# First-phase results written from the chunk's own token tile by SyncE, k.v of a batch in one run, another prologue order

## The chip, the cores and the metric

The kernel runs on one core of one Trainium2 chip. The metric is device time in microseconds (us), the median over runs. In the text PE is TensorE, PEld its weight load, DVE is VectorE, ACT is ScalarE, POOL is GpSimd and SP is SyncE; "q" behind an engine's name (SPq) means its sequencer, which issues transfers.

## The reference, cut to what matters

```python
kv  = einsum('bhsd,bhse->bhde', k, v)            # 8 batches, 8 heads, 576 tokens, 64 features
o   = einsum('bhsd,bhde->bhse', q, kv)
o   = o / sqrt(mean(o*o, -1) + 1e-6) * g_norm
x   = o as (4608 tokens, 512)
x2  = ((x @ w1) * (x @ w2)) @ w3 @ w_out         # w1, w2: 512x1024, w3: 1024x1024, w_out: 1024x512
out = silu(x2 @ w_in) @ w_out2                   # w_in: 512x2048, w_out2: 2048x512
```

The inputs q, k, v are float32, and the weights are float64, read as pairs of 32-bit words. Products of the layers are split into a high and a low float32r part and take three matmuls each.

## The kernel before

The 4608 tokens are nine chunks of 512. The core works in three stages.

- **Prologue.** w3 @ w_out is folded into one 1024x512 matrix (the tiles `wch`, `wcl`), and attention of chunk 0 and k.v of batches 0 and 1 are made beside it. The order of everything here is the string `ORDER`: each word is one load, conversion (`scale`, `tail`, `bits`, `high`, `low`), matmul group (`hh`, `hl`, `lh`, `kmm`, `a`, `b`) or copy. A `tail` is done on ACT, a `tailv` on DVE.
- **First phase** (the loop from line 834 of the kernel before). The five chunks in `PLAIN` (0, 1, 3, 5, 7) go through the first layer in steps, eight steps (j) to a chunk, 40 in all. A step is twelve matmuls into `pa`, twelve into `pb`, and twelve into four banks `x2ps` for the step before. With the last step of a chunk, which is issued during the first step of the next chunk, the four banks are copied out by ACT and DVE in turn (lines 702 and 704) and written to `x2d`. The chunk's tokens stand in `xh` and `xl`, two buffers each. Beside the steps runs the attention of the later chunks, at points that the table `TIMES` gives in sixths of a step: `l` and `q` are loads of k, v and q, `k0` and `k3` are the matmuls of k.v of one batch (tiles 0 to 2, then 3 and 4, with the copy to `kv`), `a` is q times kv, `c` to `r` are the norm, and `f0` and `f1` hand on the result: into `xh` and `xl` for a chunk of `PLAIN`, or to DRAM (`xd`) for the chunks in `LATER` (2, 4, 6, 8). `PACE` says how many pieces of the later weights are converted in each third of a step; `advance` does one, and first issues the writes that wait in the list `writes` (`flush`, line 329).
- **Second phase.** The rest, in Strassen blocks of seven products (line 924). Its tables `LATES`, `RUNS` and `NEED` set its order.

Every engine takes its instructions strictly in the order in which they are written down, and SP and POOL issue transfers in that order as well, so a transfer that has to wait for a buffer or for data holds up all behind it on the same engine. A tile has as many buffers as `bufs` says: in the kernel before `k` and `v` have three each, `q` four, and `x2o`, the tile of the copied-out results, three for four results of a chunk. The loads and most writes are on SP; the writes to `xd` and, but for the last chunk, to `x2d` are on POOL.

Of the kernel before, what the change touches and what calls it, by code (L numbers as in the profile page):

```python
# [7 lines left out]
F32 = mybir.dt.float32  # L8
F32R = mybir.dt.float32r
U32 = mybir.dt.uint32  # L10
# [5 lines left out]
P = 128  # L16
B, H, S, D = 8, 8, 576, 64
DM = H * D
# [28 lines left out]
""" if x.isdigit())  # L47
TIMES = {
# [47 lines left out]
load0 load1 load2 kload0 scale0 tail0 load3 scale1 scale2 bits0 tailv1 highv0 tailv2 bits1 low0 kmm0  # L96
high1 kload1 low1 hh1 lh1 bits2 qload0 scale3 tail3 highv2 load4 kload2 low2 kmm1 bits3 scale4
hl1 tail4 qload3 highv3 kload3 lh2 kmm2 low3 qload2 qload1 kload4 bits4 high4 hh2 hl2 low4
hl3 kmm3 kmm4 kout0 load5 scale5 tailv5 lh3 bits5 load6 a0 b0 highv5 load7 low5 scale6
tailv6 bits6 scale7 hh3 load8 tail7 highv6 low6 bits7 a1 lh5 b1 high7 load9 scale8 hh5  # L100
c0 tailv8 hl5 hl7 low7 lh7 scale9 tailv9 load10 bits8 d0 bits9 kload5 hh7 load11 high8
scale10 tailv10 low8 load12 high9 e0 hh8 lh8 low9 eh0 bits10 load13 el0 scale11 tail11 high10
bits11 hl8 hl10 r0 low10 hh10 kload6 scale12 load14 tailv12 gload0 highv11 bits12 high12 low11 x0
lh10 lh11 load15 load16 scale13 low12 tail13 r1 hh11 bits13 x1 hl11 highv13 fh0 scale14 tail14
bits14 kload7 hl13 kmm5 scale15 fh1 kmm6 low13 tailv15 scale16 lh13 kload8 hh13 wh0 wh4 wh1
highv14 bits15 low14 kmm7 kload9 high15 wl0 wl1 low15 wh5 kmm8 kmm9 tail16 wl5 lh14 kout1
bits16 hl15 hl14 wl4 fl1 hh14 lh15 hh15 highv16 low16 fl0
# [4 lines left out]
def fused(ctx, tc, q, k, v, g, w1, w2, w3t, wo1, wb, out):  # L112
# [241 lines left out]
    def kv_load(b, js):  # L354
        for j in js:
            n = min(P, S - j * P)
            for nm, src in (("k", k), ("v", v)):
                t = at.tile([P, DM], F32, tag=nm, bufs=3, name=f"{nm}{b}_{j}")
                nc.sync.dma_start(out=t[:n], in_=src[b, j * P:j * P + n, :])
                kv_t[nm, b, j] = t, n  # L360
# [3 lines left out]
    def kv_mm(b, js):  # L364
        if js[0] == 0:
            kvps[b] = bank("att", 2, f"kvps{b}")
        for j in js:
            kt, n = kv_t.pop(("k", b, j))
            vt, _ = kv_t.pop(("v", b, j))

            for p in range(KD):
                for i in range(2):
                    f = slice((2 * p + i) * D, (2 * p + i + 1) * D)
                    nc.tensor.matmul(
                        out=kvps[b][i * D:(i + 1) * D, p * D:(p + 1) * D], lhsT=kt[:n, f], rhs=vt[:n, f],
                        start=(j == 0 and p == 0), stop=(j == 4 and p == KD - 1), skip_group_check=True)

    def kv_out(b):
        nc.scalar.copy(out=kv32[b % 2], in_=kvps.pop(b)[:, :KD * D].rearrange("p (a d) -> p a d", a=KD))
# [139 lines left out]
    more = [xs.tile([P, KD, N], U32, tag=x, name=f"more_{x}").rearrange("p a n -> p (a n)") for x in ("xh", "xl")]  # L519
# [118 lines left out]
    idle = at.tile([P, N], F32, tag="x2o", bufs=3, name="idle")  # L638
# [47 lines left out]
    def g2_mm(c, j, ms):  # L686
# [6 lines left out]
        if j == K1 - 1 and ms[-1] == KD - 1:  # L693
            for m in range(KD):
                if c != PLAIN[-1]:
                    o = at.tile([P, N], F32, tag="x2o", bufs=3, name=f"x2o{c}_{m}")
                else:
                    if m == 0:
                        o4 = xs.tile([P, KD, N], F32, tag="xh", name=f"x2o{c}")
                    o = o4[:, m, :]  # L700
# [4 lines left out]
                (nc.gpsimd if c != PLAIN[-1] else nc.scalar).dma_start(out=x2d[c][:, m, :], in_=o)  # L705
# [513 lines left out]
```

## Time and profile before

| | us |
|---|---|
| median of 3 runs | 1397.71 |
| lowest, highest run | 1390.48, 1399.27 |
| the profiled execution | 1394.57 |
| its span, first to last instruction | 1392.8 |
| PE busy in it | 1369.9 (98%) |
| DVE, ACT, POOL busy | 870.8, 660.1, 347.4 |

The page of the profile gives shares over the whole span. PE is busy nearly all of it, so what can be read from the trace are the few stretches in which PE waits or in which its clock is granted at less than full. Matmul ends are modelled and overlap, so the pace of matmuls is read from their starts.

### The profile page before, as it was taken

The page shows a single profiled execution, that of the slowest core. Times are in us where ns is not written, and L with a number is a line of the kernel's source. Part 1 is how long each engine was busy: PE and PEld are TensorE (multiplying, and loading weights), DVE is VectorE, ACT ScalarE, POOL GpSimd, SP SyncE. Part 2 cuts the span into 40 slices and gives each one's busy share as a digit, 9 for nine tenths or more (in the row PEclk, how much of TensorE's full clock was granted, in tenths as well). Part 3 has the DMA queues.
Part 4 walks back from the last instruction along what each step waited for, and adds up shares of the span by engine and source line. Part 5 has one row for each costly group of instructions (what it writes and reads, how often), then busy time and mean ns, then how long its engine had stood idle before and what let it go on. Part 6 is the DMA issues. An engine that isn't in the chain of part 4 may idle for free.

```text
span 1392.8 us, 19229 instructions
## 1 busy us (share of the span) xinstructions
PE 1369.9 (98%) x7012; PEld 1143.4 (82%) x7012; DVE 870.8 (63%) x1227; ACT 660.1 (47%) x1032; POOL 347.4 (25%) x238
## 2 busy tenths in 40 slices
PE   7999999999999999999999999999999999999998
PEld 4777777776777888887888888888888889999998
DVE  5955477475774547766764677455754576567468
ACT  5767455463662425514644354544534353543543
POOL 1000100001002040522522444224522352245222
PEclk9999999999999999999999999999999999999999
DMA  9854689897868497798688667866696668888886
GB/s 365 312 191 137 212 279 328 278 316 258 274 222 290 134 312 251 231 326 267 195 269 290 192 196 227 282 192 191 193 301 197 191 207 301 279 254 268 284 254 200
DMA packets 156109, 346.26 MB, mean 249 GB/s; under 512 B 15088, under 2 KB 73456, under 8 KB 156016
## 3 DMA queue, kind: packets, MB, share of 16 engines
q1 hardware_dynamic: 152880, 335.60, 74.5%
q0 software_dynamic: 2560, 8.39, 1.5%
q8 instruction: 56, 0.92, 0.3%
q10 hardware_dynamic: 576, 1.05, 0.2%
q14 instruction: 37, 0.30, 0.1%
HBM read 270.53 MB, written 74.45 MB: 248 GB/s over the span
## 4 chain that ended last, share of the span: by engine, by line
PE 83%; issue 12%; DMA 3%; DVE 1%; ACT 1%; POOL 0%; SPq 0%; DVEq 0%; POOLq 0%; ACTq 0%
PE ps L924 65%; PE wps L608 3%; PE x2ps L150 2%; PE pb L150 2%; PE pb L152 2%; PE pa L150 1%; PE pb L151 1%; PE pa L151 1%; PE pa L152 1%; PE x2ps L151 1%; PE x2ps L152 1%; DMA x2d<-x2o 1%; DMA v<-v_l 1%; DMA more_xl<-wo_l 1%; PE o L406 1%
## 5 line engine op out<-in xcount | busy, mean ns | idle before, releaser
L924 PE MATMUL ps<-xo,w 128*128 128x512 f32 (+1 forms) x2352 | 501.4, 373 | 1.1 <-ACT u L999 1.1
L924 PEld LDWEIGHTS ps<-xo,w 128*128 128x128 f32 x2352 | 431.9, 188 | 67.2 <-ACT u L999 1.5
L924 PE MATMUL ps<-go,w 128*128 128x512 f32 (+1 forms) x2016 | 425.4, 371 | 0.4 <-issue 0.4
L924 PEld LDWEIGHTS ps<-go,w 128*128 128x128 f32 x2016 | 368.7, 188 | 53.4 <-issue 1.0
L816 DVE TENSOR_TENSOR go<-g,go 128x1024 fp32r<-128x1024 f32 (+1 forms) x120 | 136.9, 1143 | 114.5 <-ACT go L815 113.5
L934 DVE TENSOR_TENSOR c<-ps,c 128x512 f32<-128x512 f32 (+1 forms) x280 | 171.2, 639 | 57.6 <-PE ps L924 56.9
L815 ACT CAST go<-g 128x1024 fp32r<-128x1024 f32 (+1 forms) x120 | 115.1, 980 | 49.5 <-PE ps L924 48.3
L803 POOL TENSOR_TENSOR g_t<-g 128x1024 f32<-128x1024 f32 (+1 forms) x48 | 111.1, 2315 | 75.3 <-DVE g L1006 70.4
L803 POOL TENSOR_TENSOR g<-g,g_t 128x1024 f32<-128x1024 f32 (+1 forms) x24 | 53.2, 2215 | 287.7 <-DVE go L816 287.7
L816 DVE TENSOR_TENSOR go<-g_t,go 128x1024 fp32r<-128x1024 f32 (+1 forms) x48 | 81.5, 1698 | 19.7 <-ACT go L815 19.7
L956 ACT COPY s<-ps 128x512 f32<-128x512 f32 (+1 forms) x40 | 21.7, 544 | 143.9 <-PE ps L924 143.9
L934 DVE TENSOR_TENSOR g<-ps,s 128x512 f32<-128x512 f32 (+1 forms) x48 | 30.2, 643 | 66.8 <-PE ps L924 60.7
L150 PE MATMUL x2ps<-ch,wch 128*128 128x512 f32 x160 | 65.4, 409 | 5.3 <-DVE x2o L702 5.3
L857 DVE TENSOR_TENSOR asb<-pb,asb 128x512 f32<-128x512 f32 x40 | 27.5, 688 | 65.9 <-PE pb L152 65.9
L150 PE MATMUL pa<-xh,w12h 128*128 128x512 f32 x160 | 65.0, 407 | 0.1
L151 PE MATMUL pa<-xl,w12h 128*128 128x512 f32 x160 | 63.9, 399 | 0.0
L152 PE MATMUL pa<-xh,w12l 128*128 128x512 f32 x160 | 63.8, 398 | 0.0
L146 DVE TENSOR_TENSOR cl<-asb,ch 128x512 fp32r<-128x512 f32 x40 | 28.2, 706 | 56.3 <-ACT ch L145 56.3
L150 PE MATMUL pb<-xh,w12h 128*128 128x512 f32 x160 | 63.0, 394 | 0.0
L152 PE MATMUL pb<-xh,w12l 128*128 128x512 f32 x160 | 62.5, 390 | 0.4 <-DVE w12l L268 0.4
L152 PE MATMUL x2ps<-ch,wcl 128*128 128x512 f32 x160 | 62.8, 392 | 0.0
L151 PE MATMUL x2ps<-cl,wch 128*128 128x512 f32 x160 | 62.7, 392 | 0.0
(141 smaller groups left out, 1734.1 us busy)
## 6 DMA issues: line engine op xcount, KB each, us to landing
w<-wbd SPq DMA_DIRECT2D x364, 512.0 KB, 4.3
wbd<-bh SPq DMA_DIRECT2D x60, 256.0 KB, 3.5
raw<-wb_l SPq DMA_DIRECT2D x24, 512.0 KB, 5.3
wbd<-s SPq DMA_DIRECT2D x48, 256.0 KB, 3.2
q<-q_l SPq DMA_DIRECT2D x36, 256.0 KB, 4.9
k<-k_l SPq DMA_DIRECT2D x32, 256.0 KB, 5.7
v<-v_l SPq DMA_DIRECT2D x32, 256.0 KB, 5.9
raw<-w_l SPq DMA_DIRECT2D x14, 512.0 KB, 4.8
```

Source lines behind the costliest of these rows:

```text
L146: nc.vector.tensor_sub(out=l, in0=x, in1=h.bitcast(F32))
L150: nc.tensor.matmul(out=ps_out, lhsT=ah, rhs=bh, start=first, stop=False)
L151: nc.tensor.matmul(out=ps_out, lhsT=ah, rhs=bl, start=False, stop=False)
L152: nc.tensor.matmul(out=ps_out, lhsT=al, rhs=bh, start=False, stop=last)
L608: nc.tensor.matmul(out=wps[m], lhsT=(l if which == "lh" else h)[:, x:x + P], rhs=rhs, start=left[m] == all_of, stop=left[m] == 1)
L803: nc.gpsimd.tensor_tensor(out=x, in0=x if a == place else self.src[a], in1=x if b == place else self.src[b], op=ALU.subtract)
L815: nc.scalar.copy(out=t[:, 0, :, :self.w], in_=x)
L816: self.cuts[n].tensor_tensor(out=t[:, 1, :, :self.w], in0=x, in1=t[:, 0, :, :self.w].bitcast(F32), op=ALU.subtract)
L857: nc.vector.tensor_mul(out=asb, in0=pb, in1=asb)
L924: mm = lambda a, bb, start, stop: nc.tensor.matmul(out=o, lhsT=a, rhs=bb, start=start, stop=stop, skip_group_check=True)
L934: eng.tensor_tensor(out=out_, in0=a, in1=b, op=ALU.add)
L956: nc.scalar.copy(out=t[nm, d], in_=o)
```

## The change

1. **Results of the first phase.** `x2o` is gone. The four results of a chunk are copied into one tile `xo` of 128x4x512, which takes the buffer of the chunk's own `xh`. So that this can be, `xh` is no longer two turning buffers but two named ones, `xh0` and `xh1`, used by the chunks of `PLAIN` in turn. The writes to `x2d` go into the list `writes`, and so to SP with the next `flush`, not to POOL. The last chunk's stay on ACT.
2. **Attention results of the later chunks.** The writes to `xd` go from POOL to SP.
3. **k.v.** The host packs the last 64 rows of k and of v of a batch into one array `kv4` of 128x512: heads 0 to 3 in the upper 64 partitions, 4 to 7 in the lower, k on the left and v on the right. It is one load in place of two of half the size. The matmuls of a batch write two banks in place of one, ACT copies them out in two copies of 128x128 in place of one of 128x256, and in the first phase the five tiles' matmuls stand together (`k`) and not in two places (`k0`, `k3`). `k` and `v` have four buffers, and there is one for `kv4`.
4. **Orders.** `ORDER`, `TIMES` and `PACE` are other tables. `PACE` has the same sum of pieces in other places.

The diff, cut to its core:

```diff
 TIMES = {
-    "f0": (24, 43, 70, 106, 124, 186, 178, 213),
+    "f0": (22, 40, 73, 105, 128, 149, 178, 207),
-    "f1": (25, 46, 72, 95, 127, 160, 182, 213),
+    "f1": (27, 43, 79, 105, 129, 153, 182, 204),
-    "a": (2, 27, 57, 81, 111, 135, 165, 182),
+    "a": (8, 27, 57, 80, 111, 135, 164, 182),
...
-    "r": (15, 39, 69, 93, 123, 147, 177, 212),
-    "k0": (5, 43, 72, 98, 125, 151, 170),
-    "k3": (25, 52, 79, 107, 134, 158, 188),
-    "l0": (0, 16, 67, 84, 119, 142, 175),
+    "r": (21, 39, 69, 99, 122, 147, 177, 201),
+    "k": (25, 43, 78, 105, 128, 163, 176),
+    "l0": (8, 31, 39, 78, 120, 129, 154),
...
-    "q0": (19, 28, 64, 87, 120, 138, 173),
-    "q1": (15, 27, 65, 102, 117, 147, 171),
-    "q2": (15, 35, 56, 97, 123, 151, 176),
-    "q3": (18, 29, 62, 90, 117, 158, 171),
+    "q0": (3, 31, 60, 91, 121, 142, 172),
+    "q1": (9, 29, 63, 100, 109, 148, 172),
+    "q2": (2, 35, 60, 99, 114, 157, 179),
+    "q3": (16, 21, 52, 89, 111, 157, 166),
 }
...
-load0 load1 load2 kload0 scale0 tail0 load3 scale1 scale2 bits0 tailv1 highv0 tailv2 bits1 low0 kmm0
+load0 scale0 load1 load2 kload0 tail0 scale1 kmm0 kload1 load3 bits0 scale2 tail1 bits1 tail2 highv0
...
     def kv_load(b, js):
         for j in js:
-            n = min(P, S - j * P)
             for nm, src in (("k", k), ("v", v)):
-                t = at.tile([P, DM], F32, tag=nm, bufs=3, name=f"{nm}{b}_{j}")
-                nc.sync.dma_start(out=t[:n], in_=src[b, j * P:j * P + n, :])
+                if j < 4:
+                    t = at.tile([P, DM], F32, tag=nm, bufs=4, name=f"{nm}{b}_{j}")
+                    nc.sync.dma_start(out=t, in_=src[b, j * P:(j + 1) * P, :])
...
+            if j == 4:
+                t = at.tile([P, DM], F32, tag="kv4", name=f"kv{b}_{j}")
+                nc.sync.dma_start(out=t, in_=kv4[b])
...
     def kv_mm(b, js):
         if js[0] == 0:
-            kvps[b] = bank("att", 2, f"kvps{b}")
+            kvps[b] = [bank("att", 2, f"kvps{b}_{x}") for x in range(2)]
...
     def kv_out(b):
-        nc.scalar.copy(out=kv32[b % 2], in_=kvps.pop(b)[:, :KD * D].rearrange("p (a d) -> p a d", a=KD))
+        for x, y in enumerate(kvps.pop(b)):
+            nc.scalar.copy(out=kv32[b % 2][:, 2 * x:2 * x + 2, :], in_=y[:, :P].rearrange("p (a d) -> p a d", a=2))
...
         if c in LATER:
             for p in ps_:
-                nc.gpsimd.dma_start(out=xd[c][:, p, :], in_=o_t.pop((c, p)))
+                nc.sync.dma_start(out=xd[c][:, p, :], in_=o_t.pop((c, p)))
             return
         if i == 0 and part != 1:
-            xt[c] = (xs.tile([P, KD, N], F32R, tag="xh", name=f"xh{c}"),
+            xt[c] = (xs.tile([P, KD, N], F32R, tag=f"xh{PLAIN.index(c) % 2}", bufs=1, name=f"xh{c}"),
...
             for m in range(KD):
-                if c != PLAIN[-1]:
-                    o = at.tile([P, N], F32, tag="x2o", bufs=3, name=f"x2o{c}_{m}")
-                else:
-                    if m == 0:
-                        o4 = xs.tile([P, KD, N], F32, tag="xh", name=f"x2o{c}")
-                    o = o4[:, m, :]
+                if m == 0:
+                    xo = xs.tile([P, KD, N], F32, tag=f"xh{PLAIN.index(c) % 2}", bufs=1, name=f"xo{c}")
+                o = xo[:, m, :]
                 if m % 2:
                     nc.vector.tensor_copy(out=o, in_=x2ps[c][m])
                 else:
                     nc.scalar.copy(out=o, in_=x2ps[c][m])
-                (nc.gpsimd if c != PLAIN[-1] else nc.scalar).dma_start(out=x2d[c][:, m, :], in_=o)
+                if c == PLAIN[-1]:
+                    nc.scalar.dma_start(out=x2d[c][:, m, :], in_=o)
+                else:
+                    writes.append(dict(out=x2d[c][:, m, :], in_=o))
...
-        "k0": lambda c: kv_mm(c, [0, 1, 2]), "k3": lambda c: (kv_mm(c, [3, 4]), kv_out(c)),
+        "k": lambda c: (kv_mm(c, range(5)), kv_out(c)),
```

What the tables move is shown by the order of instructions at three places.

On SP, at the start of the program, the kernel before has (the name before the arrow is the tile that is loaded; `wraw` and `more` are weights, and `k_1` is tile 1 of k of batch 0):

```order
L533 DMA wraw_209<-w3t_l 128x768
L359 DMA k_0_211<-k_l 128x512
L359 DMA v_0_213<-v_l 128x512
L533 DMA more_xh<-w3t_l 128x1536
L359 DMA k_1_244<-k_l 128x512
L359 DMA v_1_246<-v_l 128x512
L383 DMA q_0_259<-q_l 128x512
L533 DMA more_xl<-wo_l 128x1024
L359 DMA k_2_269<-k_l 128x512
L359 DMA v_2_271<-v_l 128x512
L383 DMA q_3_290<-q_l 128x512
L359 DMA k_3_295<-k_l 128x512
```

The changed kernel has there:

```order
L541 DMA wraw_211<-w3t_l 128x768
L358 DMA k_0_213<-k_l 128x512
L358 DMA v_0_215<-v_l 128x512
L358 DMA k_1_231<-k_l 128x512
L358 DMA v_1_233<-v_l 128x512
L541 DMA more_xh_196<-w3t_l 128x1536
L358 DMA k_2_249<-k_l 128x512
L358 DMA v_2_251<-v_l 128x512
L541 DMA more_xl<-wo_l 128x1024
L358 DMA k_3_293<-k_l 128x512
L358 DMA v_3_295<-v_l 128x512
L362 DMA kv_4_326<-kv_l 128x512
```

The second pair of k and v goes ahead of the weights `more_xh`, and the four q tiles, which stood between the others, come behind all of k and v; the weights that follow have two q tiles fewer ahead of them (`wraw` of w_out, the next but one, comes before the last two).

On POOL, the writes of the first results of the first phase (chunk 0, `x2d_82`) stand in the kernel before between writes of attention results:

```order
L490 DMA xd_78<-ob_3_1324 128x512
L705 DMA x2d_82<-x2o_0_1661 128x512
L705 DMA x2d_82<-x2o_1_1664 128x512
L705 DMA x2d_82<-x2o_2_1667 128x512
L705 DMA x2d_82<-x2o_3_1670 128x512
L490 DMA xd_79<-ob_2_2206 128x512
```

In the changed kernel POOL has none of these, and they stand on SP:

```order
L358 DMA k_0_1496<-k_l 128x512
L358 DMA v_0_1498<-v_l 128x512
L497 DMA xd_78<-ob_0_1306 128x512
L497 DMA xd_78<-ob_1_1318 128x512
...
L328 DMA wbd_91<-s_15_1537 128x2x256
L390 DMA q_3_1710<-q_l 128x512
L328 DMA x2d_82<-xo_1705 128x512 x4
L328 DMA wbd_99<-bh_3_1792 128x2x256
L328 DMA wbd_99<-s_18_1660 128x2x256
```

Ahead of the x2d writes stands a load of q of chunk 4, which needs a buffer that the product of chunk 3 frees, and ahead of the xd writes a load of k of batch 4, which needs one that k.v of batch 3 frees.

On PE, k.v of batch 2 is in the kernel before one run of 24 matmuls and, some steps later, one of 16:

```order
L374 MATMUL kvps_954<-v_0_851,k_0_849 64x64 x8
L374 MATMUL kvps_954<-v_1_855,k_1_853 64x64 x8
L374 MATMUL kvps_954<-v_2_859,k_2_857 64x64 x8
...
L374 MATMUL kvps_954<-v_3_1033,k_3_1031 64x64 x8
L374 MATMUL kvps_954<-v_4_952,k_4_950 64x64 x8
```

The changed kernel has one run of 40, in two banks:

```order
L380 MATMUL kvps_0_1215<-v_0_996,k_0_994 64x64 x4
L380 MATMUL kvps_1_1216<-v_0_996,k_0_994 64x64 x4
L380 MATMUL kvps_0_1215<-v_1_851,k_1_849 64x64 x4
...
L380 MATMUL kvps_1_1216<-v_3_859,k_3_857 64x64 x4
L380 MATMUL kvps_0_1215<-kv_4_1027 64x64 x4
L380 MATMUL kvps_1_1216<-kv_4_1027 64x64 x4
```

The count of matmuls is the same, and the trace shows each of them as two instructions. One run in place of two stands at six batches, 2 to 7.

## Rows read from the trace of the kernel before

**Rows 1.** Windows by stage: length; busy PE, PEld, DVE, ACT, POOL; PEclk; DMA; GB/s.
```profile
0.00:72.30 72.30, 62.07 (x389) 43.98 (x390) 53.93 (x73) 45.50 (x66) 5.34 (x48) 1.00 0.93 341
72.30:468.40 396.10, 388.45 (x2258) 299.27 (x2257) 232.71 (x431) 202.10 (x369) 26.95 (x36) 0.98 0.73 243
468.40:1392.80 924.40, 919.40 (x4369) 800.15 (x4367) 584.15 (x723) 412.51 (x599) 315.13 (x154) 1.00 0.77 244
```

**Rows 2.** Waits of PE, 72.3 to 468.4: us in total, times, longest.
```profile
PE x2ps L150 <- DVE x2o L702: 5.3, 2, 3.3
...
PE rb L463 <- DVE ob L470: 0.8, 1, 0.8
```

**Rows 3.** Timeline of PE: start, us, instruction [idle before it <- what ended it].
```profile
249.82 0.50 PE L150 MATMUL x2ps<-ch,wch 128*128 128x512 f32 x1 [2.00 <-DVE x2o L702]
...
336.75 0.79 PE L150 MATMUL x2ps<-ch,wch 128*128 128x512 f32 x1 [3.30 <-DVE x2o L702]
```

**Rows 4.** Timeline of DVE just ahead of these two.
```profile
249.07 0.69 DVE L702 COPY x2o<-x2ps 128x512 f32<-128x512 f32 x1 [4.58 <-DMA x2d<-x2o]
...
336.01 0.69 DVE L702 COPY x2o<-x2ps 128x512 f32<-128x512 f32 x1 [6.74 <-DMA x2d<-x2o]
```

**Rows 5.** The granted clock behind these two, by windows (columns as in rows 1).
```profile
249.80:259.80 10.00, 9.98 (x56) 7.85 (x57) 5.70 (x11) 3.14 (x6) 1.61 (x3) 0.66 0.85 283
...
335.00:345.00 10.00, 8.24 (x24) 6.55 (x25) 3.19 (x5) 1.20 (x2) 2.67 (x5) 0.66 0.93 322
```

**Rows 6.** Timeline of PE around a run of k.v in the first phase.
```profile
191.32 0.39 PE L151 MATMUL pa<-xl,w12h 128*128 128x512 f32 x1
191.54 0.39 PE L152 MATMUL pa<-xh,w12l 128*128 128x512 f32 x1
191.86 1.62 PE L374 MATMUL kvps<-v,k 128*64 128x64 f32 x48
193.41 0.50 PE L150 MATMUL pb<-xh,w12h 128*128 128x512 f32 x1
193.75 0.39 PE L151 MATMUL pb<-xl,w12h 128*128 128x512 f32 x1
```

**Rows 7.** Timeline of PE around k.v of batch 1, in the prologue.
```profile
53.84 1.15 PE L374 MATMUL kvps<-v,k 128*64 128x64 f32 x32
54.92 1.66 PE L608 MATMUL wps<-woh,w3l 128*128 128x512 f32 x6
...
60.62 0.68 PE L374 MATMUL kvps<-v,k 64*64 64x64 f32 x16 [1.61 <-DMA v<-v_l]
61.23 0.96 PE L608 MATMUL wps<-woh,w3l 128*128 128x512 f32 x3
```

**Rows 8.** Waits of PE, 0 to 72.3.
```profile
PE kvps L374 <- DMA v<-v_l: 6.8, 5, 2.5
```

**Rows 9.** Timeline of PE in the prologue, the last tile of batch 0 and behind it.
```profile
20.87 0.68 PE L374 MATMUL kvps<-v,k 64*64 64x64 f32 x16 [0.87 <-DMA v<-v_l]
...
23.07 1.09 PE L406 MATMUL o<-q,kv 64*64 64x512 f32 x8
...
29.31 0.96 PE L608 MATMUL wps<-woh,w3l 128*128 128x512 f32 x3 [1.94 <-DVE woh L578]
```

**Rows 10.** Timeline of ACT, the conversion that `woh` comes from.
```profile
26.10 1.96 ACT L540 ACTIVATE wt<-wraw 128x1024 f32<-128x1024 f32 x2
```

**Rows 11.** The early prologue, by windows (columns as in rows 1).
```profile
10.00:20.00 10.00, 8.16 (x72) 5.80 (x72) 5.01 (x8) 3.53 (x5) 0.00 (x0) 1.00 1.06 383
```

**Rows 12.** Waits of SP's queue, 0 to 470.
```profile
SPq L329 <- ACT bh L313: 59.5, 22, 10.1
SPq L359 <- PE kvps L374: 44.1, 6, 16.0
```

**Rows 13.** Issues of v on SP: count, ns least/median/most.
```profile
L359 SPq DMA_DIRECT2D v<-v_l x40: 327/460/1214, 2.6 to 333.5; - x40
```

**Rows 14.** Waits of ACT for loads of later weights, whole span.
```profile
ACT t L209 <- DMA raw<-wb_l: 14.5, 5, 3.8
```

More of the change, by code (lines that the diff above doesn't have):

```diff
@@ L355, in kv_load @@
         for j in js:
-            n = min(P, S - j * P)
             for nm, src in (("k", k), ("v", v)):
-                t = at.tile([P, DM], F32, tag=nm, bufs=3, name=f"{nm}{b}_{j}")
-                nc.sync.dma_start(out=t[:n], in_=src[b, j * P:j * P + n, :])
-                kv_t[nm, b, j] = t, n
+                if j < 4:
+                    t = at.tile([P, DM], F32, tag=nm, bufs=4, name=f"{nm}{b}_{j}")
+                    nc.sync.dma_start(out=t, in_=src[b, j * P:(j + 1) * P, :])
+                    kv_t[nm, b, j] = t
+            if j == 4:
+                t = at.tile([P, DM], F32, tag="kv4", name=f"kv{b}_{j}")
+                nc.sync.dma_start(out=t, in_=kv4[b])
+                kv_t["k", b, j] = kv_t["v", b, j] = t
     kvps = {}
@@ L365, in kv_mm @@
         if js[0] == 0:
-            kvps[b] = bank("att", 2, f"kvps{b}")
+            kvps[b] = [bank("att", 2, f"kvps{b}_{x}") for x in range(2)]
         for j in js:
-            kt, n = kv_t.pop(("k", b, j))
-            vt, _ = kv_t.pop(("v", b, j))
+            kt, vt = (kv_t.pop((x, b, j)) for x in "kv")
             for p in range(KD):
@@ L373, in kv_mm @@
                     f = slice((2 * p + i) * D, (2 * p + i + 1) * D)
+                    r, fk, fv = slice(0, P), f, f
+                    if j == 4:
+                        r = slice(p // 2 * D, (p // 2 + 1) * D)
+                        fk, fv = (slice(y + (2 * (p % 2) + i) * D, y + (2 * (p % 2) + i + 1) * D) for y in (0, DM // 2))
                     nc.tensor.matmul(
-                        out=kvps[b][i * D:(i + 1) * D, p * D:(p + 1) * D], lhsT=kt[:n, f], rhs=vt[:n, f],
-                        start=(j == 0 and p == 0), stop=(j == 4 and p == KD - 1), skip_group_check=True)
+                        out=kvps[b][p // 2][i * D:(i + 1) * D, p % 2 * D:(p % 2 + 1) * D], lhsT=kt[r, fk], rhs=vt[r, fv],
+                        start=(j == 0 and p % 2 == 0), stop=(j == 4 and p % 2 == 1), skip_group_check=True)
     def kv_out(b):
-        nc.scalar.copy(out=kv32[b % 2], in_=kvps.pop(b)[:, :KD * D].rearrange("p (a d) -> p a d", a=KD))
+        for x, y in enumerate(kvps.pop(b)):
+            nc.scalar.copy(out=kv32[b % 2][:, 2 * x:2 * x + 2, :], in_=y[:, :P].rearrange("p (a d) -> p a d", a=2))
     def q_load(c, p):
@@ L517, in of_pair @@
         return ts[j // 2][:, (j % 2) * N:(j % 2) * N + n * N]
-    more = [xs.tile([P, KD, N], U32, tag=x, name=f"more_{x}").rearrange("p a n -> p (a n)") for x in ("xh", "xl")]
+    more = [xs.tile([P, KD, N], U32, tag=x, bufs=n, name=f"more_{x}").rearrange("p a n -> p (a n)")
+            for x, n in (("xh1", 1), ("xl", 2))]
     def wide_load(n):
@@ L637, in fused @@
     of["gload"] = g_load
-    idle = at.tile([P, N], F32, tag="x2o", bufs=3, name="idle")
+    idle = at.tile([P, N], F32, tag="ob", bufs=4, name="idle")
     nc.vector.memset(idle, 0.0)
@@ L1194, in blocks, with rows @@
         return bits(np.concatenate([a, b]))
+    def rows(x):
+        return x.transpose(0, 2, 1, 3).reshape(B, S, DM)
     arrays = {
         "q_l": lay(q.transpose(1, 3, 0, 2).reshape(KD, P, NCH, N).transpose(2, 0, 1, 3)),
-        "k_l": lay(k.transpose(0, 2, 1, 3).reshape(B, S, DM)),
-        "v_l": lay(v.transpose(0, 2, 1, 3).reshape(B, S, DM)),
+        "k_l": lay(rows(k)[:, :4 * P]),
+        "v_l": lay(rows(v)[:, :4 * P]),
+        "kv4_l": lay(np.stack([rows(x)[:, 4 * P:].reshape(B, D, 2, DM // 2) for x in (k, v)], axis=3)
+                     .transpose(0, 2, 1, 3, 4).reshape(B, P, DM)),
         "g_l": lay(g_norm),
```

24 lines of the change are left out of this document (12 added, 12 removed), and 24 rows, old and new, of tables (PACE, TIMES).

## The prediction

> **What bounds the kernel now.** I read the stages first [rows 1]. PE is the bound in all three: it is idle for 72.3 - 62.1 = 10.2 us of the prologue, for 396.1 - 388.4 = 7.7 us of the first phase, and for 5.0 us of the second phase, which the change does not touch. The reader should also see the clock column: it is 1.00 in the prologue and in the second phase, and 0.98 in the first phase alone. So what can be won is 10.2 us, 7.7 us and what the clock costs.
>
> Next, the waits of PE in the first phase [rows 2]. Two waits of x2ps for the copy of x2o make 5.3 of the 7.7 us. They are at 247.8 and 333.5 and last 2.0 and 3.3 us [rows 3]. Each ends as soon as DVE has made its second copy of a chunk's results, and DVE sat 4.58 and 6.74 us before that copy until the write of an earlier result had landed [rows 4]. x2o has three buffers for four results: the fourth copy waits for the first write. The banks x2ps are then not free for the next chunk.
>
> Then the clock behind these waits [rows 5]. Two windows of 10 us that begin at the two waits have a granted clock of 0.66, where everything else that I read is at 1.00: PE fell from 2.4 to 1.2 GHz for a while after each. A mean of 0.66 over 10 us takes 10 x 0.34 = 3.4 us of full speed, twice 6.8 us. That is dearer than the waits.
>
> Last, the prologue [rows 8]: 6.8 us in five waits of k.v for v, the longest 2.5 us, and 1.9 us for a weight [rows 9].
>
> **The change part by part.** The sum is made against the profiled execution, 1394.57 us (span 1392.8, 1.8 us around it); it is 3.1 us below the median of the runs, 1397.71.
>
> *Results into the token tile.* All four copies go to a tile of four places whose earlier content, xh of the same chunk, PE has finished reading a step before. No copy waits for a write, so both waits go: **-5.3 us** [rows 2], and with them the falls of the clock: **-6.8 us** [rows 5]. What is late next? The writes now have to land before the next chunk but one is cast into the same buffer. For chunk 0 the results are there in the ninth step (time 52 in sixths of a step), the write is issued in the tenth, and the cast of chunk 3 is at time 73; that leaves over two steps, each 36 matmuls at 0.22 us (191.32 to 191.54) [rows 6], some 16 us, against the 4.58 and 6.74 us for which DVE saw such a write in flight [rows 4]. So nothing.
>
> *Writes on SP.* 32 more transfers on SP at about 0.46 us [rows 13], 15 us of issuing in 396 us. SP spends far more than that waiting already: 59.5 us for one cast and 44.1 us for k.v, the longest 16.0 us [rows 12], and none of those waits shows up at PE. The writes of xd wait for DVE's product, which is placed between a sixth of a step and a whole one ahead of them. I put this at nothing; the cover is the prefetch of later weights three pieces ahead, and what it costs if that cover is gone is the rival on the other side below.
> The Trainium skill (DMA: Bandwidth & Descriptors, "Issuing engines are not separate DMA queues") says that issuing from several engines only saves sequencer time, since all run on the same 16 DMA engines; by that rule alone the move from POOL to SP is a loss of up to the 15 us of issuing and wins nothing, and the sum would be 15 us worse if SP were on the path. The wait of 16.0 us without a trace at PE says that it is not.
>
> *k.v in one run.* 32 instructions in a row take 54.92 - 53.84 = 1.08 us [rows 7] and 48 take 193.41 - 191.86 = 1.55 us [rows 6]: 0.47 per 16, and 0.14 fixed. Going in takes 0.32 in place of 0.22 us and coming out 0.34 [rows 6], together 0.2 more. One run less saves 0.34 us, at six batches **-2.1 us**.
>
> *Packed rows.* The last tile's 16 instructions take 61.23 - 60.62 = 0.61 us [rows 7], which is just 0.14 + 0.47: half of the rows costs what all rows cost. So the pace there is not set by how much of the array works. Between nothing and half of 0.47 at eight batches (-1.9 us) I take nothing, since this row is the operation itself but for its place.
> The Trainium skill (TensorEngine Tiling (Array Packing), "Theoretical Speedup") gives up to a factor of 2 for half the rows, which is the lower end, and the same page ("Instruction Overhead") a fixed cost per small matmul, which is the upper; the row stands with the second.
> The two copies of the result in place of one are on ACT, busy for half of the first phase (202 of 396 us) [rows 1], and the next twelve matmuls lie beside them: nothing.
>
> *Prologue.* Of the 6.8 us of waits for v, the first 2.5 us stay: the first five loads are the same. 1.6 us at 60.6 [rows 7] go or shrink: there the loads wait for buffers, and four in place of three take that away; but PE then comes sooner to the banks that the casts of `wch` free, so I take 1.3. The other 2.7 us lie before 23.1. In the changed order the q tiles, 4 x 0.26 MB, come behind all of k and v; at 383 GB/s [rows 11] the last of v lands 2.7 us earlier than at 20.87 [rows 9], and so the first product with q begins 2.7 us before 23.07. The wait for `woh` before 29.31 hangs on a conversion that ACT begins at 26.10 without having been idle [rows 10], behind that product's squares and copies, and it moves with them. So **-4.0 us**. The ends: two more conversions (`tail1`, `tail2`) go to ACT and may delay the first folded weights, so the gain may be nothing; with all waits but the first gone it would be 4.3 + 1.9 = 6.2.
>
> *The other waits of the first phase*, of 0.8 us and less [rows 2], get other places. I leave them at nothing, 2 us either way.
>
> Sum: -5.3 - 6.8 - 2.1 - 4.0 = -18.2 us, and 1394.6 - 18.2 = **1376.4 us**, 1.5% below the median.
>
> **The rivals.** One per cent of the median, about what a measurement of this kernel can tell, is 14.0 us: faster is below 1383.7, slower above 1411.7.
>
> *More goes than I count* (8%). The packed rows pass together (-1.9), the prologue loses all waits but the first (-2.2 more) and the small waits vanish (-2): 1370. For it speaks that four buffers also help batches behind the prologue; against it the row of 0.61 us.
>
> *A new wait with its clock* (15%). The new tables put work where PE waits once as it did at 333.5: 3.3 us and 3.4 us of clock. If at the same time the prologue gives nothing, the sum is -18.2 + 4.0 + 6.7 = -7.5: 1387, within 1%. For it: twelve tables are new at once, and a(5)'s norm (c, d, e all at 116) stands in one place, with DVE waiting for ACT in between. Against it: outside x2o no wait of the first phase exceeds 0.8 us [rows 2], so there is slack around all of that now.
>
> *The change does not do what it says* (5%). The copies wait for something else in place of the write, for the last reader of xh or for a write issued late, and half of the 12.1 us stays: 1382 to 1383, and with no gain in the prologue 1386 to 1387.
>
> *SP holds up the weights* (4%). Five loads stand in the new `TIMES` ahead of the matmuls that free their buffer: q of chunk 2 (2 and 3, freed at 8), of chunk 3 (21, freed at 27), of chunk 4 (52, at 57), of chunk 6 (109, at 111), and k of batch 4 (39, at 43); two pairs of xd writes (chunks 2 and 6) stand right behind their product. SP stops at each for up to a step, and the loads of later weights behind it come late; ACT, in order, stops at their conversion and then PE. If all seven cost what the wait at 333.5 cost, 6.7 us, the time is 1376.4 + 47 = 1423, slower by 1.8%. It decides from the point where a hold outlasts the three pieces that are loaded ahead. Against it: ACT waits now for such loads up to 3.8 us [rows 14] and SP for up to 16.0 us [rows 12], with no wait of PE behind either; and for two of the five holds (52 and 109) `PACE` has no piece converted until the hold is over.
>
> **How the numbers follow.** My forecast has 68%, the four rivals 8, 15, 5 and 4. Faster is the forecast and the first rival, 76%, less 2% of the forecast's own edge above 1383.7: 74%. Slower is the last rival, 4%; the rest, 22%, is within 1%. The range goes down to the first rival with 1 us of spread, 1369, and up to the second one at 1387 with 3 us, as the profiled execution lies 3.1 us below the median: 1390. Beyond it lie the last rival, the worse part of the second and third, and a little below, together under 2 in 10. The forecast's own range is 1371 to 1383, by the ends of the prologue and of the packed rows.
>
> **What would show it.** In the profile of the changed kernel, PE has no wait for the copies of x2ps, and the granted clock is 1.00 in every window after the start. The write of x2d stands on SP, and the cast into xh never waits for it. Six runs of 80 instructions take about 2.6 us each (5 x 0.47 + 0.14, and another 0.14 or so for the change to half rows), and the last tile's 16 take 0.6 us wherever they stand alone. The first phase begins about 4 us before 72.3 and lasts some 14 us less than 396.1; the second phase stays at 924 us. I am wrong if PE waits 2 us or more anywhere in the first phase, if the clock falls again, if ACT's waits for loads of later weights grow well beyond 3.8 us each, or if the prologue ends where it did.

## The result, and the profile after

The changed kernel takes 1374.8 us (median of 4 runs, 1373.18 to 1379.0), the kernel before 1394.1 in the 4 runs beside it: a ratio of 0.9865 [0.9840, 0.9889], 1.35% faster. The profiled executions stand at 1394.57 and 1374.84, 19.7 us apart; the sum had 18.2. Predicted was 1376.4, with 74% on faster. The slowest of the four changed runs, 1379.0, has a granted clock of 0.996, and the other three 0.999 to 1.0.

The stages of the kernel after, by windows that end at the first product of a stage (columns as in [rows 1], which they answer to):

```profile
0.00:68.00 68.00, 62.95 (x388) 44.23 (x389) 51.78 (x69) 45.18 (x68) 5.01 (x48) 1.00 0.95 364
68.00:449.00 381.00, 378.43 (x2257) 293.79 (x2257) 235.66 (x433) 203.33 (x378) 10.78 (x4) 1.00 0.74 252
449.00:1373.10 924.10, 919.83 (x4369) 800.39 (x4367) 585.76 (x723) 412.78 (x599) 315.28 (x154) 1.00 0.75 244
```

The prologue lost 4.3 us and the first phase 15.1; the second phase kept its 924. In the first phase PE is idle for 381.00 - 378.43 = 2.6 us instead of 7.7, and the clock column reads 1.00 instead of 0.98. PE's busy time fell by 388.45 - 378.43 = 10.0 us: this is the clock and the matmuls of k.v together, which the experiments separate.

All waits of PE in the first phase (us in total, times, longest; against [rows 2]):

```profile
PE rb L470 <- DVE rhl L460: 0.9, 1, 0.9
PE pa L149 <- ACT asb L860: 0.8, 1, 0.8
PE rb L470 <- DVE asb L865: 0.4, 1, 0.4
PE pb L151 <- DVE w12l L267: 0.3, 1, 0.3
```

No x2ps is left, and nothing lasts 1 us. The longest of the prologue (against [rows 8, 9]):

```profile
PE kvps L380 <- DMA v<-v_l: 1.9, 3, 0.9
PE idle_ps L650 <- DVE idle L647: 1.5, 1, 1.5
PE o L413 <- DMA q<-q_l: 1.1, 1, 1.1
PE wps L616 <- DVE w3l L599: 0.5, 1, 0.5
```

k.v waits 1.9 us instead of 6.8, and the 1.94 us for woh are gone; a wait of 1.1 for q is new. Not all of the 4.9 us is gain: the first product of k.v waits 0.85 us instead of 2.50, but it begins at 8.85 instead of 9.29, since the eight matmuls on `idle` ahead of it took 6.54 us in this execution and 5.33 in the one before. The first product with q begins at 20.02 instead of 23.07.

A run of k.v in the first phase, and behind the dots the packed tile of batch 0, which stands alone (timeline of PE; against [rows 6, 7]):

```profile
107.07 2.08 PE L380 MATMUL kvps<-v,k 128*64 128x64 f32 x64
109.09 0.47 PE L380 MATMUL kvps<-kv 64*64 64x64 f32 x16
109.49 0.50 PE L149 MATMUL pb<-xh,w12h 128*128 128x512 f32 x1
...
18.03 0.47 PE L380 MATMUL kvps<-kv 64*64 64x64 f32 x16
18.43 0.50 PE L616 MATMUL wps<-woh,w3l 128*128 128x512 f32 x1
```

The 64 full instructions take 109.09 - 107.07 = 2.02 us, which is 4 x 0.47 + 0.14 as the sum had it. The 16 packed ones take 0.40, both times, where the last tile took 0.61. A run of 80 is 2.42 us, not 2.63.

Waits of SP's queue up to the second phase (against [rows 12]):

```profile
SPq L390 <- PE o L413: 49.0, 4, 19.4
SPq L328 <- ACT bh L312: 33.5, 22, 6.1
...
SPq L358 <- PE kvps L380: 14.7, 3, 11.6
```

The writes of x2d on that queue (count, ns least/median/most, first and last start; against [rows 13]):

```profile
L328 SPq DMA_DIRECT2D x2d<-xo x16: 326/406/1012, 163.0 to 392.4; - x16
```

ACT's waits for loads of weights in the whole span (against [rows 14]):

```profile
ACT t L208 <- DMA raw<-wb_l: 4.0, 3, 2.0
```

SP stops longest at loads of q (L390) that stand ahead of the matmuls that free their buffer, up to 19.4 us; the loads of weights behind them are not late for ACT (4.0 us instead of 14.5).

### The profile page after: what moved, and what is told of

Read it like the earlier page. It is cut to its first block, busy times and chain, and to the rows that moved or that the text cites. A ratio compares the mean times of both kernels' runs of the same rounds, so it can differ in the third digit from the quotient of the medians.

```text
span 1373.1 us, 19202 instructions
## 1 busy us (share of the span) xinstructions
PE 1361.2 (99%) x7012; PEld 1138.4 (83%) x7012; DVE 873.2 (64%) x1225; ACT 661.3 (48%) x1042; POOL 331.1 (24%) x206
## 3 DMA queue, kind: packets, MB, share of 16 engines
q10 hardware_dynamic: 576, 1.05, 0.2%
## 4 chain that ended last, share of the span: by engine, by line
PE 93%; DMA 3%; ACT 1%; DVE 1%; SPq 1%; issue 1%; ACTq 0%; DVEq 0%
PE ps L932 66%; PE wps L616 3%; PE x2ps L149 3%; PE pb L149 2%; PE pb L151 2%; PE pa L149 2%; PE pb L150 2%; PE x2ps L150 2%; PE pa L150 2%; PE pa L151 2%; PE x2ps L151 2%; PE kvps L380 1%; PE o L413 1%; DMA k<-k_l 1%; DMA q<-q_l 1%; PE s L432 1%
## 5 line engine op out<-in xcount | busy, mean ns | idle before, releaser
L811 POOL TENSOR_TENSOR x_t<-x2r 128x1024 f32<-128x1024 f32 (+1 forms) x14 | 32.5, 2322 | 420.1 <-DMA w<-wbd 419.6
## 6 DMA issues: line engine op xcount, KB each, us to landing
wbd<-bh SPq DMA_DIRECT2D x60, 256.0 KB, 3.9
wbd<-s SPq DMA_DIRECT2D x48, 256.0 KB, 4.1
q<-q_l SPq DMA_DIRECT2D x36, 256.0 KB, 5.1
k<-k_l SPq DMA_DIRECT2D x32, 256.0 KB, 5.2
v<-v_l SPq DMA_DIRECT2D x32, 256.0 KB, 5.3
```

Source lines behind the costliest of these rows:

```text
L811: nc.gpsimd.tensor_tensor(out=x, in0=x if a == place else self.src[a], in1=x if b == place else self.src[b], op=ALU.subtract)
```

## The experiments

The theory to start from was that of the prediction: the writes of x2o with three buffers cost two waits and two falls of the clock, the token tile takes both away, and the queue that issues the writes does not matter. The rivals: the queue does it, or the waits only make room for others. Unless it is said otherwise, ratios are to the kernel before, in runs on the same chip.

**The tile alone.** The kernel before, with the first phase's results in a tile of four places that takes turns with xh (two tiles of the prologue, `idle` and `more`, move to other buffers for it):

```diff
-            xt[c] = (xs.tile([P, KD, N], F32R, tag="xh", name=f"xh{c}"),
+            xt[c] = (xs.tile([P, KD, N], F32R, tag=f"xh{PLAIN.index(c) % 2}", bufs=1, name=f"xh{c}"),
...
-                    o = at.tile([P, N], F32, tag="x2o", bufs=3, name=f"x2o{c}_{m}")
...
+                    xo = xs.tile([P, KD, N], F32, tag=f"xh{PLAIN.index(c) % 2}", bufs=1, name=f"xo{c}")
+                o = xo[:, m, :]
```

> The kernel before with one part of the change: a chunk's four results are copied into the buffer of its own token tile, and the writes stay on POOL, at once after each copy. Theory (the three buffers of x2o are the cause): PE has no wait for x2o (5.3 us before), the granted clock is 1.00 throughout the first phase, and the time is 12 us below the kernel before, a ratio of 0.990 to 0.993. Rival (the order on POOL is the cause, writes of results behind writes of attention): the waits and both falls of the clock stay, ratio 0.998 to 1.002.

1389.24 us, ratio 0.9974 [0.9959, 0.9990]: 4 us, not 12, and between the two expectations. The waits for x2o are gone, but the waits of PE in the first phase tell of another:

```profile
PE kvps L374 <- DMA v<-v_l: 2.4, 1, 2.4
PE pa L150 <- ACT asb L850: 1.0, 2, 0.7
```

Its place in the timeline of PE:

```profile
340.24 1.30 PE L374 MATMUL kvps<-v,k 128*64 128x64 f32 x32 [2.41 <-DMA v<-v_l]
```

The window behind it (columns as in [rows 1]):

```profile
342.00:345.40 3.40, 3.40 (x9) 2.63 (x9) 2.86 (x7) 2.54 (x5) 0.00 (x0) 0.51 0.15 45
```

Next to the place of the longer wait for x2o (336.75 in [rows 3]) PE now waits 2.41 us for v of batch 7, and for 3.4 us in the stretch behind it the clock is at 1.2 GHz. In the kernel before, the last load of that batch was issued at 333.49 and landed 6.1 us later, at about 340. PE waited for x2o until 336.75, then ran some 6 us at 1.2 GHz, and came to this product only at 345.89: the wait and the slow clock behind it together had hidden the late load. The whole first phase of the tile alone:

```profile
75.00:463.90 388.90, 383.32 (x2258) 295.82 (x2257) 234.66 (x431) 202.03 (x369) 28.15 (x36) 1.00 0.73 247
```

In the profiled execution the phase is 7.2 us shorter than before, not 12.1: the wait for v takes back 2.4, half-speed for 3.4 us another 1.7, and the other waits are 1.0 longer. The rest of the way down to 4 us over the runs lies outside the first phase or between executions (the prologue took 75.0 us here) and was not divided up.

**The queue alone.** Three buffers of x2o kept, the writes on SP:

```diff
-                (nc.gpsimd if c != PLAIN[-1] else nc.scalar).dma_start(out=x2d[c][:, m, :], in_=o)
+                (nc.sync if c != PLAIN[-1] else nc.scalar).dma_start(out=x2d[c][:, m, :], in_=o)
```

> The kernel before with the writes of the first-phase results issued on SP in place of POOL, at once after each copy, x2o still with three buffers. Theory (the buffers): the fourth copy still waits for the first write to land, PE waits 3 to 8 us for it and the clock falls once or more; ratio 0.996 to 1.004. Rival (the queue): the waits are gone and the ratio is 0.990 to 0.993.

1392.41 us, 0.9994 [0.9978, 1.0009]. The wait stays (waits of PE, first phase):

```profile
PE x2ps L150 <- DVE x2o L702: 4.7, 1, 4.7
```

One place holds 4.7 us, against 5.3 at two places before. So the wait for x2o comes with the three buffers on either queue.

**Four and two buffers of x2o.** The kernel before with another number; for four, tensors that only pad the memory were left out.

```diff
-                    o = at.tile([P, N], F32, tag="x2o", bufs=3, name=f"x2o{c}_{m}")
+                    o = at.tile([P, N], F32, tag="x2o", bufs=4, name=f"x2o{c}_{m}")
```

> The kernel before with four buffers for x2o in place of three (the unused padding tiles are left out to make room). Theory: the same as with the token tile, no wait of PE for x2o, clock 1.00, ratio 0.990 to 0.993. Rival (the queue on POOL): waits and falls stay, ratio 0.998 to 1.002.

> The kernel before with two buffers for x2o: the suspected wait is made larger, the third and fourth copies wait for a landing. Theory: PE waits for x2o at three or four chunk ends, 8 to 18 us in all, with a fall of the clock behind each wait of 2 us or more (3.4 us each, three or four of them); ratio 1.006 to 1.014. Rival 1 (the queue on POOL): no change, ratio 0.998 to 1.002. Rival 2 (the falls of the clock have another cause than these waits): the waits grow but the falls stay two, ratio 1.002 to 1.007.

Four: 1391.29 us, 0.9987 [0.9972, 1.0002]. That is in the range of the rival (0.998 to 1.002) and not of the theory, but not by the rival's mechanism, since the waits for x2o are gone. Two: 1399.94, 1.0053 [1.0034, 1.0073], slower, but below the 1.006 to 1.014 of the theory and in the range of the second rival (the waits grow, the falls of the clock do not). The timeline of PE with four:

```profile
338.49 1.30 PE L371 MATMUL kvps<-v,k 128*64 128x64 f32 x32 [3.18 <-DMA v<-v_l]
```

The window behind that wait, with the clock at 1.00:

```profile
338.50:342.00 3.50, 3.50 (x42) 2.99 (x43) 1.24 (x3) 1.72 (x4) 0.00 (x0) 1.00 0.32 111
```

The waits of PE for x2ps with two buffers:

```profile
PE x2ps L150 <- ACT x2o L704: 6.0, 2, 4.4
PE x2ps L150 <- DVE x2o L702: 1.1, 1, 1.1
```

The window behind the longest of them:

```profile
337.20:340.60 3.40, 3.40 (x9) 2.44 (x8) 2.71 (x5) 2.03 (x4) 2.90 (x6) 0.50 1.01 369
```

With four the wait for x2o turns into the same wait for v; with two it grows to 7.1 us, and only the longest of its three waits has a fall of the clock behind it in the profiled execution, where the theory had three or four falls. The number of buffers works on the waits in the expected direction. That each wait brings its fall of the clock is not borne out, and with four most of the gain is given back at one place.

**Is the late v a matter of buffers?** A new question, with two theories: k and v have three buffers, so their loads are issued late; or the batch is used too early after loads that land late. First the tile and a fourth buffer (the diff is to the tile alone):

```diff
-                t = at.tile([P, DM], F32, tag=nm, bufs=3, name=f"{nm}{b}_{j}")
+                t = at.tile([P, DM], F32, tag=nm, bufs=4, name=f"{nm}{b}_{j}")
```

> The kernel before with the token tile and with four buffers in place of three for k and for v; old ORDER, TIMES and PACE, k.v in two places, rows unpacked, writes on POOL. In the run with the token tile alone PE then waited 2.4 us for v at 337, where loads of batch 7 that wait for a buffer land late, and the clock fell behind it. Theory (the wait for x2o had hidden late loads, and the third buffer makes them late): with four buffers no wait of PE for v above 1 us in the first phase, no fall of the clock there, first phase 383 to 386 us, ratio 0.989 to 0.993. Rival (they are late by their place in TIMES and by crowded DMA queues, not by the buffers): the wait of 2 to 3 us stays, ratio 0.996 to 0.999.

1388.58 us, 0.9968 [0.9949, 0.9986]. The wait stays. The first phase:

```profile
71.00:459.10 388.10, 381.93 (x2257) 294.82 (x2256) 235.35 (x433) 202.66 (x371) 28.14 (x36) 1.00 0.74 248
```

The timeline of SP, with the loads of batch 7:

```profile
324.62 1.32 SPq L359 DMA_DIRECT2D v<-v_l  x1
326.04 1.28 SPq L359 DMA_DIRECT2D k<-k_l  x1
327.36 1.27 SPq L359 DMA_DIRECT2D v<-v_l  x1
```

The product that needs them, in the timeline of PE:

```profile
336.68 1.30 PE L374 MATMUL kvps<-v,k 128*64 128x64 f32 x32 [3.28 <-DMA v<-v_l]
```

A window from the loads to that product:

```profile
322.00:338.00 16.00, 12.72 (x88) 10.11 (x83) 4.87 (x8) 4.20 (x8) 4.30 (x8) 1.00 0.99 339
```

The loads of v between 300 and 360, and their time to landing:

```profile
L359 SPq DMA_DIRECT2D v<-v_l x4: 447/862/1322, 304.3 to 327.4; - x4
...
DMA to landing us min/median/max: 3.4/6.7/10.1
```

The loads go out at 324.6 and 327.4, into a stretch where the DMA engines are busy at 0.99, and one of them takes 10.1 us to land. The buffers theory fell. Then the batch used four sixths of a step later (a sixth is 1.6 us here), and nothing else (to the kernel just above):

```diff
-    "k3": (25, 52, 79, 107, 134, 158, 188),
+    "k3": (25, 52, 79, 107, 134, 162, 188),
```

> As e6_tile_four_buffers (token tile, four buffers, old tables), with one number of TIMES moved: the second run of k.v of batch 7 from 158 to 162 sixths of a step. In e6 PE waited 3.3 us there for v; the loads are issued seven sixths ahead and take 9 us to land, with the DMA engines busy 0.99 of the time. Theory (the wait is the place of the use, and the loads land meanwhile): no wait of PE for v above 1 us in the first phase, which takes 384 to 386 us in place of 388.1; ratio 0.992 to 0.9955. Rival (the DMA engines are the limit there, and the wait goes over to q or to the next in the queue): first phase 387 to 389 us, ratio 0.996 to 0.998.

1381.68 us, 0.9913 [0.9892, 0.9934]: 6.9 us below the kernel just above, from one number (the two ran on different chips; by their ratios it is 7.7 us). The first phase takes 384.9 us, in the range; the ratio is a hair beyond it, on the fast side. PE's waits of 0.4 us and more in the first phase:

```profile
PE rb L463 <- DVE asb L855: 0.8, 2, 0.4
PE rb L463 <- DVE ob L470: 0.8, 1, 0.8
PE pb L152 <- DVE w12l L268: 0.4, 1, 0.4
```

None is for v. The whole phase in one window, with the clock at 1.00:

```profile
69.70:454.60 384.90, 382.47 (x2258) 295.00 (x2257) 237.72 (x433) 202.59 (x371) 27.29 (x36) 1.00 0.75 250
```

Of the 6.9 us, 3.2 are the first phase of the two profiled executions. Much of the rest is the clock, which the profiled execution of the kernel just above happens not to show: over the runs of each, what the clock takes, (1 - clock) x span, has a median of 4.2 us there and 0.7 with the batch used later. So the place of use decided, given these loads. The later use without the tile or without the fourth buffer was not run.

In the changed kernel the same batch has both, a later use (163) and earlier loads: the last load of v of that batch goes out at 300.44 and its run begins at 331.59, 31 us later (timeline, SP and PE):

```profile
300.44 0.42 SPq L358 DMA_DIRECT2D v<-v_l  x1
...
331.59 2.08 PE L380 MATMUL kvps<-v,k 128*64 128x64 f32 x64
```

**The prologue.** The changed kernel with the order of before, and the kernel before with the changed one. Of twelve lines of the table the first:

```diff
-load0 scale0 load1 load2 kload0 tail0 scale1 kmm0 kload1 load3 bits0 scale2 tail1 bits1 tail2 highv0
+load0 load1 load2 kload0 scale0 tail0 load3 scale1 scale2 bits0 tailv1 highv0 tailv2 bits1 low0 kmm0
...
```

> The changed kernel with the prologue's ORDER of the kernel before; all else as changed (four buffers, packed rows, TIMES, PACE, token tile, writes on SP). Theory (the order brings k and v earlier): the first phase begins about 2.7 us later than in the changed kernel and is the same from there, ratio to the kernel before 0.988 to 0.990 where the changed kernel has 0.9865. Rival 1 (four buffers and the single load of the packed rows do all that the prologue gains): 0.985 to 0.9875. Rival 2 (the order does far more than the sum says, since the token tile alone gave 4 us and not 12): 0.992 or more.

> The kernel before with the new ORDER of the prologue alone. Theory: the first phase begins 2 to 3.5 us earlier than the mean of 73.0 us that five profiled runs with the old order and three buffers have (71.1 to 75.0), and keeps its waits for x2o; ratio 0.997 to 0.999. Rival (with three buffers the new order stops at the loads of tile 3 and later, and the gain needs the fourth): 1.000 or more.

The first: 1378.18 us, 0.9880 [0.9856, 0.9905], 3.4 us above the changed kernel's median in another set of runs; its first phase begins at 71.0 instead of 68.0, and takes 380.8. The second: 1394.83, 1.0002 [0.9985, 1.0019]; prologue 71.7, and the waits for x2o still there:

```profile
PE x2ps L150 <- DVE x2o L702: 7.0, 2, 4.0
```

So the order is worth 3.0 us in this pair, with four buffers and the packed load, and without them no gain is seen; the interval leaves room for 2 us. The pair agrees with its neighbours. With the new order and four buffers the first phase begins at 67.8 to 68.3 in five kernels (the changed one and four of its variants), with the old order and four buffers at 69.7 to 71.0 in three.

**The writes back on POOL.** The changed kernel, with xd and x2d issued by POOL:

```diff
-                nc.sync.dma_start(out=xd[c][:, p, :], in_=o_t.pop((c, p)))
+                nc.gpsimd.dma_start(out=xd[c][:, p, :], in_=o_t.pop((c, p)))
...
-                    writes.append(dict(out=x2d[c][:, m, :], in_=o))
+                (nc.gpsimd if c != PLAIN[-1] else nc.scalar).dma_start(out=x2d[c][:, m, :], in_=o)
```

> The changed kernel with the writes of attention results and of first-phase results back on POOL, at once after their copies. Theory (the queue costs and wins nothing): ratio to the kernel before 0.985 to 0.988, no new wait of PE above 1 us. Rival 1 (the writes on SP hold up loads): faster than the changed kernel, below 0.985, with shorter waits of SP for DVE. Rival 2 (the move off POOL is where the rest of the gain is from): 0.990 or more.

1374.9 us, 0.9861 [0.9841, 0.9881]; prologue 68.0, first phase 380.4. The expectation of no new wait above 1 us failed (waits of PE, first phase):

```profile
PE pa L149 <- ACT asb L857: 1.6, 1, 1.6
```

In the changed kernel this wait is 0.8 us. In time nothing of it is seen: within the interval the queue neither costs nor wins.

**One half of the array.** The changed kernel, with every matmul of the packed tile on the upper 64 rows, so that the lower 64 rows are left out of the product:

```diff
-                        r = slice(p // 2 * D, (p // 2 + 1) * D)
+                        r = slice(0, D)
```

> The changed kernel, but all matmuls of the packed last tile read its upper 64 partitions; the lower 64 rows are left out of the product. Theory (the two halves of the rows pass beside one another): the 16 instructions of the last tile take 0.6 us in place of 0.40 and a run of 80 takes 2.6 in place of 2.42 us. Rival (the two banks, or the place behind the other tiles, make them faster): 0.40 and 2.42 us remain.

One run, 1375.35 us. The timeline of PE where the run above stood at 107.07:

```profile
108.32 0.68 PE L380 MATMUL kvps<-kv 64*64 64x64 f32 x16
108.94 0.50 PE L149 MATMUL pb<-xh,w12h 128*128 128x512 f32 x1
```

The same 16 instructions take 0.62 us instead of 0.40, close to the 0.61 of [rows 7]. So two halves side by side pass together. The first phase:

```profile
68.30:449.20 380.90, 379.51 (x2258) 295.09 (x2257) 236.71 (x433) 203.83 (x377) 10.78 (x4) 1.00 0.74 252
```

PE is busy 1.1 us longer than in the changed kernel (six times 0.22 would be 1.3), but the phase is not longer, 380.9 us against 381.0: PE is idle for 1.4 us instead of 2.6. So the packing saves busy time, and that it saves time is not shown by this one run.

**Early loads of q.** The changed kernel with the times of q of before:

```diff
-    "q0": (3, 31, 60, 91, 121, 142, 172),
-    "q1": (9, 29, 63, 100, 109, 148, 172),
...
+    "q0": (19, 28, 64, 87, 120, 138, 173),
+    "q1": (15, 27, 65, 102, 117, 147, 171),
...
```

> The changed kernel with the times of the q loads of the kernel before, which stand behind the matmuls that free their buffers. Theory (the early q loads hold SP and cost nothing): first phase 380 to 382 us as in the changed kernel (381.0), though SP's waits for the product with q fall from 49 us to under 15. Rival 1 (the holds cost PE time): first phase below 379.5. Rival 2 (q comes late without them): above 383.

One run, 1373.05 us. The first phase in one window:

```profile
68.00:446.90 378.90, 378.15 (x2258) 294.14 (x2257) 236.15 (x433) 203.19 (x377) 10.77 (x4) 1.00 0.75 253
```

SP's wait at the loads of q:

```profile
SPq L390 <- PE o L413: 18.3, 2, 9.9
```

The hold on SP falls from 49.0 to 18.3 us (under 15 was expected), PE's idle time from 2.6 to 0.8, and the phase from 381.0 to 378.9, in the range of the first rival. This points to some 2 us that the early loads cost. The changed kernel's own runs go down to 1373.18, so one run does not settle it.

**A try at the waits that are left.** The changed kernel with a1 later in the order, two small steps a sixth later, one piece of weight moved on to the next third of its step in PACE, and the packed products in the order 0, 2, 1, 3:

```diff
-201 021 000 100 122 140 200 020
+201 021 000 100 122 140 110 020
...
-    "f0": (22, 40, 73, 105, 128, 149, 178, 207),
+    "f0": (23, 40, 73, 105, 128, 149, 178, 207),
...
-    "r": (21, 39, 69, 99, 122, 147, 177, 201),
+    "r": (22, 39, 69, 99, 122, 147, 177, 201),
```

> The changed kernel with its four largest remaining waits attacked: the second product with q of chunk 0 behind one more group of weight matmuls (1.05 us), the spread of chunk 1 one sixth later (0.88), one of two pieces in a third of step 14 moved on (0.85), and the packed rows' matmuls in the order upper, lower, upper, lower (0.40 us per batch now). Theory (each wait is slack of its own): 2.5 to 3 us off, ratio to the kernel before 0.983 to 0.9855. Rival (the engine that was late there stays late, and each wait comes back behind it): 0.986 to 0.988, and the last tile's 16 instructions stay at 0.40 us.

1375.4 us, 0.9863 [0.9845, 0.9882]: nothing won, as the rival had it. The two longest waits of the first phase, 0.9 and 0.8 us, are gone, and one of 1.68 us stands elsewhere, with a clock of 0.50 behind it. The timeline of PE:

```profile
104.07 0.54 PE L149 MATMUL pa<-xh,w12h 128*128 128x512 f32 x1 [1.68 <-DVE ob L477]
```

The window that begins just behind that wait:

```profile
104.40:107.80 3.40, 3.40 (x9) 2.64 (x8) 3.31 (x6) 2.38 (x4) 0.00 (x0) 0.50 0.00 0
```

The order of the packed products did not matter: 0.39 us at the packed tile of batch 0, against 0.40.

## Why the prediction was right, point by point

**x2o and the clock behind it, -12.1 predicted.** Right in sum for the change, wrong in what it rested on. The step said that nothing is late next; it looked at the writes alone. The tile alone gives 4 us, since v of batch 7 lands 2.4 to 3.3 us late just there (3.18 with four buffers of x2o, 3.28 with four of k and v). Only with that batch also used later does the ratio reach 0.9913: 0.87% of the 1394.73 us of before beside it, 12.1 us [9.2, 15.1], a fourth buffer included. So the 12.1 us belong to the tile and to the distance between the loads of that batch and their use together. The new tables have that distance, with 31 us; the prediction did not know that it was needed, so that the step came out in full was luck. What the new tables would give with x2o kept was not run. In the profiled first phases: idle time went from 7.7 (before) to 6.2 (tile, four buffers) to 2.4 (and used later), while PE's busy time went from 388.45 to 381.93 to 382.47. The fall of the busy time is the clock: 6.5 us of the 6.8 in the sum. (The second window of [rows 5] begins 1.75 us ahead of the wait's end, and part of its slow clock lies in idle time.)

That clock term was taken from an execution that had more of it than most. Over the 54 runs of the kernel before that stood beside the experiments, the granted clock goes from 0.994 to 0.999 and the time with it: ten runs at 0.999 have a median of 1389.99 us, sixteen at 0.995, the clock of the profiled one, 1394.82. What the clock takes, (1 - clock) x span, has a median of 5.6 us over the 54, against 7.0 in the profiled execution. In eight runs of the changed kernel and its twin with the writes on POOL it is 1.2 on average, most of it 5.5 us in the one run at 0.996. Over runs the clock gave back some 4 to 5 us, not 6.8.

**k.v in one run, -2.1, and the packed rows, 0.** The row of 0.61 us is of a tile that stands on the upper half alone; the one-half kernel shows 0.62 and the changed one 0.40. The packed rows were mis-sized by 0.21 us at eight batches, 1.7 us of PE's busy time, close to the end of the range (-1.9). In the first phase six runs at 0.34 + 0.21 give 3.3; PE's busy time falls by 381.93 - 378.43 = 3.5 from the kernel with tile and four buffers to the changed one, or by 4.0 from the one with the later use. The one-half kernel divides this: 1.1 is the packing, and the other 2.4 to 3.0 go with the joined runs (2.1 predicted), which had no run of their own. In time the packing was not seen to save anything, as the one-half kernel shows. The Trainium skill (TensorEngine Tiling (Array Packing), "Theoretical Speedup") gives up to a factor of 2 for half the rows. Here the trace agrees: less the fixed 0.14 us, 0.26 in place of 0.48, a factor of 1.8. The prediction had sided with the other rule of that page.

**Prologue, -4.0.** 72.3 to 68.0, -4.3. By parts: 3.0 for the order (2.7 predicted), and 71.0 in place of 72.3 for the buffers and the packed load (1.3 predicted). The first part shows in the timelines too: with the old order the first product with q begins at 22.01 instead of 20.02, and the wait of 1.95 us for woh is there instead of the 1.05 for q, together 2.9 us. The second part is shown in its sign only. Five kernels with the old order and three buffers begin the first phase at 71.1 to 75.0 in their one profiled execution each, three with the old order and four buffers at 69.7 to 71.0. Alone the order gave 0.6 us, which is within that scatter; the prediction had not said that it needs the buffers.

**Writes on SP, 0.** Right: 1374.9 with them on POOL. The early loads of q, which the prediction had only as a rival on the slower side, may cost 2 us. The rival's own way did not come: ACT's waits for loads of later weights fell from 14.5 to 4.0 us. A wait of ACT for its own buffer `bh` until a write had landed is new, 4.6 us in four, the longest 2.6, and no long wait of PE stands behind it.

**Small waits, 0, and the second phase, 0.** Small waits went from 7.7 - 5.3 = 2.4 us to 2.6 in the first phase. The second phase is 924.1 us against 924.4.

Sum of the profiled executions: -4.3 - 15.1 - 0.3 = -19.7. The forecast's -18.2 is 1.5 short. That is about the 1.7 us of busy time that it lacked for the packed rows, but since the one-half kernel is as fast in its one run, the 1.5 us cannot be put down to them. It is also within the 5.8 us between the changed kernel's own four runs.

**The rivals.** A new wait with its clock did not come in the profiled execution of the changed kernel, where no wait of the first phase exceeds 0.9 us; its run with a clock of 0.996, 1379.0 us, was not profiled. It did come in the tile alone, which lacks the new tables. It was the right rival, but for the part and not the whole. Of "more goes than I count" one item of three came, the packed rows, in busy time; the small waits did not vanish, and the prologue gained 4.3 us, not 6.2.

## What to carry to other kernels

A wait that is taken away hides the one behind it: before a stall is counted as gain, look at the loads that land inside it and at how late they would be without it. A term for the clock should be taken over the clocks of several runs, not from the one execution that was profiled. Half-height matmuls are to be priced from a trace with both halves in flight, since a row with one half says nothing of them.

## What the runs showed of the hardware

- Sixteen instructions of 64x64 matmuls on 64 rows each take 0.40 us when eight of them are on either half of the array, and 0.62 when all are on the same half.
- The length of one wait does not tell whether the clock falls. Behind waits of 1.68, 2.41 and 4.4 us PE ran at 1.2 GHz for about 3.4 us (windows of 0.50 and 0.51 above), and behind waits of 3.18 and 3.28 us at 2.4 (a window of 1.00 above; in the kernel with tile and four buffers 128x512 products at a pitch of 0.23 us right behind it). With two buffers of x2o a wait of 1.69 us had no fall either (clock 1.00 from 251.2 to 256.0). What else decides was not tried.
- The same kernel does not get the same clock in every run: over 54 runs of the kernel before, 0.994 to 0.999, with medians of 1396.1 and 1390.0 us at the two ends.
- At a DMA share of 0.99 a load of 0.26 MB took up to 10.1 us to land; one of the same size, issued at 300.44 in the changed kernel at a share of 0.86 (298 to 306), took 4.3.
